# Attention, experts and MLP on one core: Strassen's scheme on two chunks of 320 tokens for seven expert blocks

## The chip, the cores and the metric

The kernel runs on one core of one Trainium2 chip. The metric is the device time of one execution in microseconds (us). The change is compared with the kernel before by the medians of several runs of each on one chip.

## The reference, cut to what matters

```python
# q, k, v: (2, 8, 576, 64)
scores = scale * q @ k.T + decay          # causal, decay from cumsum(log f)
x = softmax(scores) @ v                   # -> x: 1152 tokens x 512
p = domain_probs / domain_probs.sum(-1, keepdims=True)
for e in range(4):                        # experts, w1: 512 x 1024, w2: 1024 x 512
    out += p[:, e:e+1] * (np.maximum(x @ w1[e], 0) @ w2[e])
h = out @ w_in                            # w_in: 512 x 2048, w_out: 2048 x 512
y = (h * (1 / (1 + np.exp(-1.702 * h)))) @ w_out
```

All of it is wanted to float32 accuracy. The two MLP weights arrive as 64-bit floats; the others as float32.

## The kernel before, in words

**Products.** Each float32 operand is split into a rounded high part and the rest: `x` into `xh`, `xl`, a first-layer weight into `whi`, `wlo`, a hidden value into `hh`, `hl`. A product is then three passes of matmuls: high by high, low by high, high by low. `whi` and `hh` are rounded by ScalarE (ACT, the helper at L56), `wlo` is a subtraction on VectorE (DVE, L208).

**Blocks and visits.** The hidden units come in 12 blocks of 512: eight of the experts (0 to 7, two for each) and four of the MLP (8 to 11). `visits` lists which block goes over which chunks of tokens in which order. While attention still runs, visits 0 to 9 do blocks 2, 1, 0 and 3 on the four chunks that attention delivers (256, 256, 256 and 384 tokens). Visits 7, 8 and 9 are blocks 3, 1 and 0 on the last two of them, tokens 512 to 1151. Visits 10 to 17 are blocks 4 to 11 on three chunks of 384 (`WIDE`).

**Units.** `seq` lists units of work. Kind 1 is a plain first layer of a block on a chunk (`emit_l1`, L800): four steps of 12 matmuls. Kind 2 is the second layer (`emit_l2`, L914): per tile of 128 tokens 12 matmuls that are 512 wide, whose result DVE adds to `acc` (L925 for experts, L931 and L934 for the MLP). Kind 3 is half of a first layer of two chunks together by Strassen's scheme (`emit_joint`, L839): seven products of six matmuls where the plain way has eight. It needs sums of weights and sums of tokens. The sums of weights (`sr`) are four operations of POOL for each half (L224 to L227), split by `split_sums` into `sh` (ACT, two operations) and `sl` (DVE, L237, two operations). The pool `ws` holds one such pair. The sums of tokens are ten additions `tr` (L260), four roundings `th` (ACT) and four subtractions `tl` (L255); `sum_tokens` makes them twice, once for the experts (all additions on POOL, spread over visits 7 to 9) and once for the MLP (seven on DVE, three on POOL, in visit 14). In visits 10 to 13 and 15 to 17 the order is: half 0, the second layer left over from the visit before, half 1, the third chunk plainly, and the second layer of the first two chunks. Visit 14, the MLP's first, is plain, since its input is only just made: `split_output` transposes each finished tile on the PE (L1037) and splits it into `xh` and `xl` (L1043).

**After a product.** The first layer of an expert ends in `jc` (DVE, L844), a relu, `hh` (ACT) and `hl` (POOL, L848); that of the MLP in a gelu (ACT, L902), `hh` and `hl` (DVE, L904).

**MLP weights.** `mlp_convert` turns the 64-bit floats into float32, 32 tiles, each by six DVE operations (L313 to L327, on tiles `cvt`, `cvd`, `wf`). The result is stored to DRAM (`wm`, L340) and loaded again as `wst` (L62) when its block is due. `cv_due` sets how many of these steps go with each unit step.

**Order.** A scheduler orders the PE's instructions. From visit 10 on `pin_turn` fixes the order of DVE, ACT and POOL as the program emits it. These three engines and each DMA queue work in their order: an instruction that waits holds up all behind it.

Of the kernel before, what the change touches and what calls it, by code (L numbers as in the profile page):

```python
# [23 lines left out]
WN = 384  # L24
WIDE = [NCH, NCH + 1, NCH + 2]
# [5 lines left out]
TS_FROM, TS_EVERY = 7, 2  # L31
# [4 lines left out]
def attn_moe_mlp(ctx: ExitStack, tc: tile.TileContext, qk0, qk1, qk2, v0, vp, fg, dp, wa_moe, wb_moe, wa_mlp, wb_mlp, out):  # L36
# [34 lines left out]
    h_p = pool("h", 2)  # L71
# [68 lines left out]
    runs = [[v_ for v_, (b, cs) in enumerate(visits) if cs is WIDE and lo <= b < hi]  # L140
            for lo, hi in ((0, NMOE), (NMOE + 1, NBLK))]
    joint = runs[0] + runs[1]
    for run in runs:
        at = seq.index((1, run[0], visits[run[0]][0], WIDE[0]))
        ends = run[-1] + 1 == len(visits)
        to = len(seq) if ends else seq.index((1, run[-1] + 1, visits[run[-1] + 1][0], WIDE[0]))
        mid, before = [], seq[at + 1]
        for v_ in run:
            b = visits[v_][0]
            mid += [(3, v_, b, WIDE[0]), before, (3, v_, b, WIDE[1]), (1, v_, b, WIDE[2]), (2, v_, b, WIDE[0]), (2, v_, b, WIDE[1])]  # L150
            before = (2, v_, b, WIDE[2])
        seq[at:to] = mid + [before] * ends
    v8 = runs[0][-1] + 1
    ts_units = [(2, v8 - 1, NMOE - 1, WIDE[2]), (1, v8, NMOE, WIDE[1]), (2, v8, NMOE, WIDE[0])]
    last_unit = {v_: cs[-1] for v_, (b, cs) in enumerate(visits)}
# [85 lines left out]
    def sum_tokens(eng, eng3):  # L241

        (h11, h21, h12, h22), (l11, l21, l12, l22) = ([t[c][:, k:k + 2] for c in WIDE[:2] for k in (0, 2)] for t in (xh, xl))
        if not ts:
            th, tl = (late["ts"].tile([128, 4, 2, WN], F32R, name=n) for n in ("th", "tl"))
            ts.update({n: (th[:, n - 1], tl[:, n - 1]) for n in range(1, 5)})
            ts.update({11: (h11, l11), 21: (h21, l21), 22: (h22, l22)})
        ra, rb = (late["jr"].tile([128, 1024], F32, tag="jr", name="tr")[:, :2 * WN].rearrange("p (k n) -> p k n", k=2)
                  for _ in range(2))
# [19 lines left out]
        sub_, add_ = eng3.tensor_sub, eng3.tensor_add  # L269
# [13 lines left out]
    v_mlp = [v_ for v_, (b, _) in enumerate(visits) if b >= NMOE]  # L283
    m_order = [(k, v_, g) for v_ in v_mlp for k in "ab" for g in range(4)]
# [108 lines left out]
    def load_plain(h0):  # L393
# [394 lines left out]
    hbuf = {}  # L788

    def emit_l1(v_, b, c, g):  # L790
        n = span[c][1]
        if g == 0:
            hbuf[v_, c] = (h_p.tile([128, 4, WN], F32R, tag="hh", name="hh"),
                           h_p.tile([128, 4, WN], F32R, tag="hl", name="hl"))
        hh, hl = hbuf[v_, c]
# [33 lines left out]
    def emit_joint(v_, b, m):  # L829

        c1, c2 = WIDE[:2]
        for c, p in ((c1, h_p), (c2, late["h2"])) if m == 0 else ():
            hbuf[v_, c] = tuple(p.tile([128, 4, WN], F32R, tag=t, name=t) for t in ("hh", "hl"))
        (h1, l1), (h2, l2) = hbuf[v_, c1], hbuf[v_, c2]
# [61 lines left out]
    def evac_l1(b, n, g, hh, hl, p):  # L896
        if b < NMOE:
            nc.scalar.activation(out=hh[:, g, :n], in_=p[:, :n], func=AF.Relu)  # L898
            nc.vector.scalar_tensor_tensor(out=hl[:, g, :n], in0=p[:, :n], scalar=0.0, in1=f(hh[:, g, :n]),  # L899
                                           op0=ALU.max, op1=ALU.subtract)  # L900
# [4 lines left out]

    def emit_l2(v_, b, c, j):

# [4 lines left out]
        for i, (x, w) in enumerate([(hh, 0), (hh, 1), (hl, 0)]):
            for k in range(4):
                nc.tensor.matmul(p, lhsT=x[:, k, o], rhs=wb[v_, k][w].rearrange("p a c -> p (a c)"),  # L914
                                 start=(i == 0 and k == 0), stop=(i == 2 and k == 3))
        return lambda: evac_l2(v_, b, c, t, p)
# [280 lines left out]
```

## Time and profile before

| | us |
|---|---|
| runs | 702.04, 700.75, 701.94 (median 701.94) |
| the profiled execution | 699.91 |
| its span in the profile | 698.2 |
| PE busy in it | 686.4 (98%) |
| DVE busy in it | 493.3 (71%) |
| ACT, POOL busy in it | 326.3, 212.7 |

The span is that of the instructions of one execution; the execution's own time is 1.71 us longer. PE is TensorE, PEld its weight loads. A matmul's busy time in a timeline overlaps its neighbours'; the chain of waits gives the time that a run of matmuls really took.

### The profile page before, as it was taken

Reading aid. Unit: us, or ns where it says so; the run is one execution under the profiler, and the core shown is the slowest. Engines: PE = TensorE matmul, PEld = TensorE weight load, DVE = VectorE, ACT = ScalarE, POOL = GpSimd, SP = SyncE. Lnnn points to the kernel's source line nnn. Section 1 sums busy time; section 2 is a strip of 40 time slices with the busy share of each in tenths; the row PEclk is TensorE's granted clock in tenths of the full one; section 3 lists DMA queues with packets and bytes.
Section 4 is the critical chain, followed back from the end, with each engine's and each line's share of the span. In section 5 each row is a group of like instructions: output and inputs, shape, how many; then the busy total and the mean of one; then the engine's idle time right before and its main releaser. Section 6 shows DMA issues by size and latency. Waiting matters only on the chain.

```text
span 698.2 us, 10644 instructions
## 1 busy us (share of the span) xinstructions
PE 686.4 (98%) x3864; PEld 608.3 (87%) x3865; DVE 493.3 (71%) x1004; ACT 326.3 (47%) x737; POOL 212.7 (30%) x237
## 2 busy tenths in 40 slices
PE   8999999999999999999999999999989999999997
PEld 4797888888888998999899898897988898998986
DVE  6896776676486777657877679677876779684632
ACT  5777766676441342346045244352455453451430
POOL 6887566632260033015116025120043302100000
PEclk9999999999999999999999999999999999999999
DMA  7686735332323614413413343234103244110012
GB/s 260 232 288 242 271 118 190 127 92 92 121 61 107 209 50 163 107 45 114 143 55 127 121 134 104 95 121 150 46 18 117 77 152 152 45 61 31 0 46 91
DMA packets 38597, 83.37 MB, mean 119 GB/s; under 512 B 3560, under 2 KB 3568, under 8 KB 38544
## 3 DMA queue, kind: packets, MB, share of 16 engines
q1 hardware_dynamic: 38504, 82.65, 35.9%
q8 instruction: 30, 0.49, 0.3%
q14 instruction: 23, 0.19, 0.1%
q10 hardware_dynamic: 40, 0.04, 0.0%
HBM read 71.88 MB, written 10.78 MB: 118 GB/s over the span
## 4 chain that ended last, share of the span: by engine, by line
PE 95%; DVE 2%; POOL 1%; ACT 1%; DMA 1%; issue 0%; SPq 0%; POOLq 0%
PE m L914 42%; PE m L800 25%; PE m L839 15%; PE s L536 4%; PE x L640 4%; PE t L610 3%; DMA dpraw<-in_dp_dram 1%; DVE tr L260 0%; POOL ks L462 0%; PE m L1037 0%; PE m L817 0%; POOL e L592 0%; PE t L684 0%; PE m L953 0%; ACT xh L56 0%; POOL qlo L480 0%
## 5 line engine op out<-in xcount | busy, mean ns | idle before, releaser
L914 PE MATMUL m<-whi,hh 128*128 128x512 f32 x432 | 119.4, 392 | 0.0
L914 PE MATMUL m<-wlo,hh 128*128 128x512 f32 x432 | 117.1, 391 | 0.0
L914 PE MATMUL m<-whi,hl 128*128 128x512 f32 x432 | 116.3, 390 | 0.0
L208 DVE TENSOR_TENSOR wlo<-wst,whi 128x512 fp32r<-128x512 f32 x140 | 110.4, 806 | 4.8 <-ACT whi L56 4.3
L56 ACT ACTIVATE whi<-wst 128x512 fp32r<-128x512 f32 x144 | 85.9, 625 | 28.5 <-PE m L914 17.8
L914 PEld LDWEIGHTS m<-whi,hl 128*128 128x128 f32 x432 | 80.9, 188 | 17.1
L914 PEld LDWEIGHTS m<-wlo,hh 128*128 128x128 f32 x432 | 80.9, 188 | 17.0
L914 PEld LDWEIGHTS m<-whi,hh 128*128 128x128 f32 x432 | 79.7, 188 | 13.7
L800 PE MATMUL m<-xh,whi 128*128 128x384 f32 (+1 forms) x400 | 79.4, 315 | 2.6 <-ACT xh L56 2.6
L800 PE MATMUL m<-xh,wlo 128*128 128x384 f32 (+1 forms) x400 | 78.7, 313 | 0.0
L800 PE MATMUL m<-xl,whi 128*128 128x384 f32 (+1 forms) x400 | 78.6, 313 | 0.0
L800 PEld LDWEIGHTS m<-xh,whi 128*128 128x128 f32 x400 | 65.0, 189 | 4.9 <-ACT xh L56 3.3
L848 POOL TENSOR_TENSOR hl<-jc,hh 128x384 fp32r<-128x384 f32 x24 | 24.5, 1020 | 139.9 <-ACT hh L56 139.9
L800 PEld LDWEIGHTS m<-xh,wlo 128*128 128x128 f32 x400 | 65.1, 189 | 0.0
L800 PEld LDWEIGHTS m<-xl,whi 128*128 128x128 f32 x400 | 64.7, 189 | 0.3
L592 POOL TENSOR_SCALAR e<-e,sm 128x128 f32<-128x128 f32 (+4 forms) x72 | 46.0, 650 | 54.4 <-DVE sm L590 25.2
L898 ACT ACTIVATE hh<-m 128x256 fp32r<-128x256 f32 (+1 forms) x84 | 36.0, 428 | 55.1 <-PE m L800 55.0
L899 DVE SCALAR_TENSOR_TENSOR hl<-m,hh 128x256 fp32r<-128x256 f32 (+1 forms) x84 | 40.6, 483 | 29.5 <-ACT hh L898 28.9
L925 DVE SCALAR_TENSOR_TENSOR acc<-m,dpn,acc 128x512 f32<-128x512 f32 x63 | 47.0, 746 | 17.5 <-PE m L914 17.3
L904 DVE TENSOR_TENSOR hl<-m,hh 128x384 fp32r<-128x384 f32 x48 | 26.7, 555 | 32.6 <-ACT hh L56 32.5
L582 ACT ACTIVATE e<-e,mx 128x128 f32<-128x128 f32 (+4 forms) x72 | 41.6, 580 | 11.1 <-DVE mx L566 10.6
L902 ACT ACTIVATE m<-m 128x384 f32<-128x384 f32 x48 | 23.1, 481 | 39.5 <-DVE m L844 37.8
(142 smaller groups left out, 1147.3 us busy)
## 6 DMA issues: line engine op xcount, KB each, us to landing
wst<-in_wa_moe_dram SPq DMA_DIRECT2D x28, 512.0 KB, 4.4
wst<-in_wb_moe_dram SPq DMA_DIRECT2D x28, 512.0 KB, 4.2
mst<-in_wa_mlp_dram SPq DMA_DIRECT2D x16, 512.0 KB, 3.9
wm<-wf SPq DMA_DIRECT2D x32, 256.0 KB, 3.4
mst<-in_wb_mlp_dram SPq DMA_DIRECT2D x16, 512.0 KB, 4.0
wst<-wm SPq DMA_DIRECT2D x16, 512.0 KB, 3.8
cb<-cumd SPq DMA_DIRECT2D x16, 256.0 KB, 4.0
qr<-in_qk_dram SPq DMA_DIRECT2D x8, 384.0 KB, 5.4
```

The costliest lines, as they stand in the source:

```text
L56: return nc.scalar.activation(out=out, in_=in_, func=AF.Copy)
L208: (nc.gpsimd if v_ == 0 and kind == 'a' and g < 4 else nc.vector).tensor_sub(lf, raw, f(hf))
L536: nc.tensor.matmul(pt[:, :z - a], lhsT=lr[i][0], rhs=lr[i][1], start=i == 0 and not (both and pt is not bank), stop=i == n - 1, skip_group ...
L582: nc.scalar.activation(out=e[:, off:off + w], in_=e[:, off:off + w], func=AF.Exp, scale=-1.0, bias=mx, accum_out=sm[:, 0, k:k + 1])
L592: nc.gpsimd.tensor_scalar(out=e[:, off:off + w], in0=e[:, off:off + w], scalar1=sm[:, 0, i:i + 1], scalar2=1.0, op0=ALU.mult, op1=ALU.mult)
L640: nc.tensor.matmul(pt[64 * g:64 * g + 64, o:n], lhsT=lhsT, rhs=rhs, start=i == 0, stop=i == nk - 1)
L800: nc.tensor.matmul(p[:, :n], lhsT=w[:, k, :], rhs=x[c][:, k, :], start=(j == 0 and k == 0), stop=(j == 2 and k == 3))
L839: nc.tensor.matmul(p[:, :WN], lhsT=w[a][:, k, :], rhs=x[z][:, k, :], start=start and j == 0 and k == 0, stop=stop and j == 2 and k == 1, s ...
L898: nc.scalar.activation(out=hh[:, g, :n], in_=p[:, :n], func=AF.Relu)
L899: nc.vector.scalar_tensor_tensor(out=hl[:, g, :n], in0=p[:, :n], scalar=0.0, in1=f(hh[:, g, :n]), op0=ALU.max, op1=ALU.subtract)
L914: nc.tensor.matmul(p, lhsT=x[:, k, o], rhs=wb[v_, k][w].rearrange("p a c -> p (a c)"), start=(i == 0 and k == 0), stop=(i == 2 and k == 3))
L925: nc.vector.scalar_tensor_tensor(out=a, in0=p, scalar=d, in1=a, op0=ALU.mult, op1=ALU.add)
```

## The change

Visits 7, 8 and 9 become joint too, on two chunks of 320 tokens (512 to 831, 832 to 1151), and have no third chunk. Visits 10 to 13 use the same two chunks and do tokens 0 to 511 plainly as one chunk of 512 (`REST`). A new kind 4 (`emit_l2_joint`) does the second layer of the five tiles of the two chunks: first the parts of k = 0, 1 into five accumulators, then those of k = 2, 3. The MLP keeps chunks of 384 in a new order: joint are tokens 384 to 1151, plain are 0 to 383. Its first visit begins with tokens 768 to 1151. The last expert's tokens 0 to 511 finish after the others, its tiles in the order 3, 0, 1, 2. The sums of tokens are made once per 320-token pair and once per 384-token pair, now wholly on DVE: the experts' two steps at a time in the three last units of visit 6. Fewer conversion steps go with early units (`cv_due` 0.3 instead of 0.7), and 1.2 with each later one. The buffers of `hh`, `hl` become two tiles that `h_of` cuts up. `pin_turn` begins at visit 7.

```diff
-WIDE = [NCH, NCH + 1, NCH + 2]
+JN = 320
+LATE = [(384, WN), (768, WN), (0, WN), (S - 64, JN), (S - 64 + JN, JN), (0, S - 64)]
+MLP = [NCH, NCH + 1, NCH + 2]
+EXP = [NCH + 3, NCH + 4, NCH + 5]
+REST = EXP[2]
...
-    visits = [(2, [0]), (1, [0]), (0, [0]), (3, [0, 1]), (0, [1]), (1, [1]), (2, [1, 2, 3]), (3, [2, 3]), (1, [2, 3]), (0, [2, 3])]
-    visits += [(b, WIDE) for b in range(4, NBLK)]
+    visits = [(2, [0]), (1, [0]), (0, [0]), (3, [0, 1]), (0, [1]), (1, [1]), (2, [1, 2, 3])]
...
+    v_exp, v_all, v_mlp = len(visits), len(visits) + 3, len(visits) + 7
+    visits += [(b, EXP[:2]) for b in (3, 1, 0)] + [(b, EXP) for b in range(4, NMOE)] + [(b, MLP) for b in range(NMOE, NBLK)]
+    joint = [v_ for v_ in range(v_exp, len(visits)) if v_ != v_mlp]
...
+    before = []
+    for v_ in range(v_exp, len(visits)):
+        b, cs = visits[v_]
+        if v_ == v_mlp:
+            seq += before
+            seq += [(1, v_, b, cs[1]), (1, v_, b, cs[0]), (2, v_, b, cs[1]), (1, v_, b, cs[2]), (2, v_, b, cs[0])]
+            before = [(2, v_, b, cs[2])]
+            continue
+        seq += [(3, v_, b, cs[0])] + before + [(3, v_, b, cs[1])]
+        seq += [(1, v_, b, c) for c in cs[2:]]
+        seq += [(4, v_, b, cs[0])] if b < NMOE else [(2, v_, b, cs[0]), (2, v_, b, cs[1])]
+        before = [(2, v_, b, c) for c in cs[2:]]
+    seq += before
+    sums_at = {(1,) + units[-1]: 2, (2,) + units[-2]: 2, (2,) + units[-1]: 2}
+    sums_at.update({(1, v_mlp, NMOE, MLP[0]): 2, (2, v_mlp, NMOE, MLP[1]): 2, (1, v_mlp, NMOE, MLP[2]): 1, (2, v_mlp, NMOE, MLP[0]): 1})
...
-    def sum_tokens(eng, eng3):
+    def sum_tokens(cs):
...
+        eng, width = nc.vector, span[cs[0]][1]
...
-        sub_, add_ = eng3.tensor_sub, eng3.tensor_add
...
     def emit_l2(v_, b, c, j):
...
+        if c == REST:
+            j = (3, 0, 1, 2)[j]
...
+    def emit_l2_joint(v_, b, c, j):
+
+        if j < 5:
+            both.append(ps_tile())
+            l2_products(v_, b, c, j, both[j], (0, 1))
+            return lambda: None
+        p = both[j - 5]
+        l2_products(v_, b, c, j - 5, p, (2, 3))
+        if j == 9:
+            both.clear()
+        return lambda: evac_l2(v_, b, c, span[c][0] // 128 + j - 5, p)
...
-            ts_gen = sum_tokens(nc.gpsimd, nc.gpsimd)
-        if (kind, v_, b, c) == ts_units[0]:
-            ts_gen = sum_tokens(nc.vector, nc.gpsimd)
+            ts_gen = sum_tokens(EXP)
+        u, m = (kind, v_, b, c), visits[v_][1].index(c)
+        if u == (1, v_mlp, NMOE, MLP[0]):
+            ts_gen = sum_tokens(MLP)
...
-                if (kind, v_, b, c) not in ts_units:
-                    cv_due[0] += (0.7 if v_ < 10 else 0.5 if kind == 3 else 1.4 if b >= NMOE else 1.3) * (4 / n_steps)
+                if sums_at.get(u, 0) < 2:
+                    cv_due[0] += (0.3 if v_ < v_all else 1.2) * (4 / n_steps)
...
-            if v_ >= 10:
+            if v_ >= v_exp:
                 pin_turn()
```

How the order of instructions moves, at three places. Rows are line, operation, result and operands, shape, and how many stand in a row. The changed kernel's lines are its own: L837 is the plain first layer, L874 the joint one, L950 the second layer, L1094 the transposes.

**PE, from half 0 to half 1 of the first joint visit.** Before (visit 10), from the last product of half 0:

```order
L839 MATMUL m<-xl,sh 128x384 x2
L914 MATMUL m<-whi,hh 128x512
L914 MATMUL m<-wlo,hh 128x512 x4
L914 MATMUL m<-whi,hl 128x512 x4
L914 MATMUL m<-whi,hh 128x512 x4
L914 MATMUL m<-wlo,hh 128x512 x4
L914 MATMUL m<-whi,hl 128x512 x4
L839 MATMUL m<-xh,whi 128x384 x2
L839 MATMUL m<-xh,wlo 128x384 x2
L839 MATMUL m<-xl,whi 128x384 x2
L839 MATMUL m<-th,sh 128x384 x2
```

Changed (visit 7), from the last rows of half 1's first product, which now stands ahead of half 0's last:

```order
L874 MATMUL m<-xl,whi 128x320 x2
L874 MATMUL m<-xh,sh 128x320 x2
L874 MATMUL m<-xh,sl 128x320 x2
L874 MATMUL m<-xl,sh 128x320 x2
L874 MATMUL m<-th,sh 128x320 x4
L950 MATMUL m<-whi,hh 128x512 x2
L950 MATMUL m<-wlo,hh 128x512 x2
L950 MATMUL m<-whi,hl 128x512 x2
L874 MATMUL m<-th,sh 128x320 x2
L874 MATMUL m<-th,whi 128x320 x2
```

Before, 21 second-layer matmuls of another visit and the next first product stand between the last use of one `sh` and the first use of the next. Now they follow each other directly, and behind four matmuls come six of this visit's own second layer.

**PE, from the last expert to the MLP.** Before, from the transposes of tile 1:

```order
L1037 MATMUL m<-identr,acc_79 128x128 x4
L914 MATMUL m<-whi,hh 128x512 x4
L914 MATMUL m<-wlo,hh 128x512 x4
L914 MATMUL m<-whi,hl 128x512 x4
L1037 MATMUL m<-identr,acc_79 128x128 x4
L800 MATMUL m<-xh,whi 128x384 x4
L800 MATMUL m<-xh,wlo 128x384 x4
L1037 MATMUL m<-identr,acc_79 128x128 x4
L800 MATMUL m<-xh,whi 128x384 x4
L800 MATMUL m<-xh,wlo 128x384 x4
```

Changed, from the transposes of tile 8 on:

```order
L1094 MATMUL m<-identr,acc_2863 128x128 x4
L950 MATMUL m<-whi,hh_2861 128x512 x4
L950 MATMUL m<-wlo,hh_2861 128x512 x4
L950 MATMUL m<-whi,hl_2862 128x512 x4
L1094 MATMUL m<-identr,acc_79 128x128 x8
L837 MATMUL m<-xh,whi 128x384 x4
L837 MATMUL m<-xh,wlo 128x384 x4
L837 MATMUL m<-xl,whi 128x384 x4
```

Before, the MLP's first layer reads tiles 0 to 2, and the transposes of tile 2 stand right ahead of it. Now it reads tiles 6 to 8, and behind the last of their transposes come a tile's second layer and the transposes of two other tiles.

**DVE, the last conversions.** Before, from the last conversion step (L327) to visit 17's first `u`:

```order
L327 TENSOR_TENSOR wf<-wf,cvd 128x512
L904 TENSOR_TENSOR hl<-m,hh 128x384
L208 TENSOR_TENSOR wlo<-wst,whi 128x512
L237 TENSOR_TENSOR sl<-sr,sh 128x512 x2
L904 TENSOR_TENSOR hl<-m,hh 128x384
L208 TENSOR_TENSOR wlo<-wst,whi 128x512
L931 TENSOR_TENSOR acc_79<-m,acc_79 128x512
L208 TENSOR_TENSOR wlo<-wst,whi 128x512
L931 TENSOR_TENSOR acc_79<-m,acc_79 128x512 x4
L931 TENSOR_TENSOR acc_2876<-m,acc_2876 128x512
L867 TENSOR_TENSOR u_6960<-m,u_6960 128x384
L874 TENSOR_TENSOR u_6961<-m,u_6960 128x384
```

Changed, from the middle of visit 17's half 0 to the first `u` of its half 1:

```order
L880 TENSOR_TENSOR m<-u_7026,m 128x384
L944 TENSOR_TENSOR hl_2862<-m,hh_2861 128x384
L342 TENSOR_SCALAR cvt<-wf 128x512
L257 TENSOR_TENSOR sl<-sr,sh 128x512 x2
L880 TENSOR_TENSOR m<-m,u_7025 128x384
L944 TENSOR_TENSOR hl<-m,hh 128x384
L345 SCALAR_TENSOR_TENSOR cvd<-mst,cvt 128x512
L347 TENSOR_TENSOR wf<-wf,cvd 128x512
L988 TENSOR_TENSOR acc_79<-m,acc_79 128x512 x3
L228 TENSOR_TENSOR wlo<-wst,whi 128x512
L903 TENSOR_TENSOR u_7157<-m,u_7157 128x384
```

The last conversion stood ten rows ahead of visit 17; now the last three steps lie within its first half.

## Rows read from the trace of the kernel before

**Rows 1.** The page: span, two engines, granted TensorE clock in slices.
```profile
span 698.2 us, 10644 instructions
...
PE 686.4 (98%) x3864; PEld 608.3 (87%) x3865; DVE 493.3 (71%) x1004; ACT 326.3 (47%) x737; POOL 212.7 (30%) x237
...
PEclk9999999999999999999999999999999999999999
```

**Rows 2.** Chain of waits, 180 to 345 us: start, length, line, instructions.
```profile
199.37 8.34 PE m L800 x48
207.72 5.48 PE m L914 x24
213.20 5.75 PE m L800 x48
...
296.50 6.26 PE m L839 x36
...
306.20 1.06 PE m L839 x6
307.27 4.80 PE m L914 x21
```

**Rows 3.** Who PE waited for, 200 to 698 us: total, times, longest.
```profile
PE m L800 <- ACT xh L56: 2.6, 2, 1.9
```

**Rows 4.** Timeline of PE, 485 to 523 us: start, length, and idle before.
```profile
488.85 0.97 PE L800 MATMUL m<-xh,whi 128*128 128x384 f32 x4 [0.69 <-ACT xh L56]
...
520.06 0.97 PE L800 MATMUL m<-xh,whi 128*128 128x384 f32 x4 [1.95 <-ACT xh L56]
```

**Rows 5.** Timeline of ACT, 485 to 523 us.
```profile
517.77 0.84 ACT L56 ACTIVATE th<-tr 128x768 fp32r<-128x768 f32 x1 [4.51 <-DVE tr L260]
```

**Rows 6.** Timeline of DVE, 485 to 523 us.
```profile
499.95 0.95 DVE L260 TENSOR_TENSOR tr<-xh 128x768 f32<-128x768 f32 x1
...
515.15 2.59 DVE L260 TENSOR_TENSOR tr<-tr,xl 128x768 f32<-128x768 f32 x1
```

**Rows 7.** Timeline of POOL, 485 to 523 us.
```profile
514.76 4.66 POOL L260 TENSOR_TENSOR tr<-tr,xl 128x768 f32<-128x768 f32 x2
```

**Rows 8.** Timeline of ACT, 302 to 313 us.
```profile
307.37 1.16 ACT L56 ACTIVATE sh<-sr 128x512 fp32r<-128x512 f32 x2 [1.31 <-PE m L839]
```

**Rows 9.** Timeline of DVE, 304 to 313 us.
```profile
308.45 1.29 DVE L237 TENSOR_TENSOR sl<-sr,sh 128x512 fp32r<-128x512 f32 x2
```

**Rows 10.** Busy time of each engine in three stretches.
```profile
194.00:221.40 27.40, 27.40 (x156) 25.05 (x155) 23.69 (x33) 10.39 (x22) 9.52 (x5) 1.00 0.34 106
...
344.06:391.62 47.56, 47.56 (x241) 43.23 (x241) 36.59 (x62) 18.50 (x36) 14.16 (x14) 1.00 0.34 107
...
591.32:638.88 47.56, 47.56 (x241) 43.23 (x241) 32.59 (x59) 19.50 (x40) 2.92 (x4) 1.00 0.15 52
```

**Rows 11.** DVE groups, 543 to 640 us: busy, mean ns, idle before.
```profile
L904 DVE TENSOR_TENSOR hl<-m,hh 128x384 fp32r<-128x384 f32 x24 | 13.3, 555 | 13.6 <-ACT hh L56 13.6
L208 DVE TENSOR_TENSOR wlo<-wst,whi 128x512 fp32r<-128x512 f32 x17 | 12.2, 725 | 0.0
L931 DVE TENSOR_TENSOR acc<-m,acc 128x512 f32<-128x512 f32 x15 | 10.2, 684 | 5.7 <-PE m L914 5.7
L327 DVE TENSOR_TENSOR wf<-wf,cvd 128x512 f32<-128x512 f32 x8 | 6.4, 805 | 0.1
...
L237 DVE TENSOR_TENSOR sl<-sr,sh 128x512 fp32r<-128x512 f32 x8 | 5.2, 687 | 2.6 <-ACT sh L56 2.6
```

**Rows 12.** Busy time of the instructions on tile cvt in one stretch.
```profile
543.76:591.32 47.56, 14.07 (x23) 2.65 (x4) 1.00 0.39 135
```

**Rows 13.** Timeline of DVE, 192 to 200 us.
```profile
194.65 5.55 DVE L208 TENSOR_TENSOR wlo<-wst,whi 128x512 fp32r<-128x512 f32 x3
```

**Rows 14.** The page: DMA issues, KB each, median us to landing.
```profile
wm<-wf SPq DMA_DIRECT2D x32, 256.0 KB, 3.4
...
wst<-wm SPq DMA_DIRECT2D x16, 512.0 KB, 3.8
```

More of the change, by code (lines that the diff above doesn't have):

```diff
@@ L77, in attn_moe_mlp @@
     xh_t, xl_t = (big.tile([128, 4, NT], F32R, name=n) for n in ("xh", "xl"))
-    span = [(0, 256), (256, 256), (512, 256), (768, 384)] + [(i * WN, WN) for i in range(3)]
+    span = [(0, 256), (256, 256), (512, 256), (768, 384)] + LATE
     xh, xl = ([t[:, :, t0:t0 + n] for t0, n in span] for t in (xh_t, xl_t))
@@ L139, in attn_moe_mlp @@
     seq.append((2,) + units[-1])
[L140 to L155, printed above, removed]
+    before = []
[13 more added lines that the diff above has]
+    sums_at.update({(1, v_mlp, NMOE, MLP[0]): 2, (2, v_mlp, NMOE, MLP[1]): 2, (1, v_mlp, NMOE, MLP[2]): 1, (2, v_mlp, NMOE, MLP[0]): 1})
+    last_l1, last_l2 = {}, {}
+    for u in seq:
+        (last_l1 if u[0] in (1, 3) else last_l2)[u[1]] = u
     w_turn = [("a", 0), ("b", 0)]
-    for kind, v_, b, c in seq:
-        if c == last_unit[v_] and v_ + 1 < len(visits):
-            w_turn.append(("ab"[kind - 1], v_ + 1))
+    for u in seq:
+        if u[1] + 1 < len(visits) and u in (last_l1[u[1]], last_l2[u[1]]):
+            w_turn.append(("ab"[u[0] in (2, 4)], u[1] + 1))
     w_pairs = [(k, v_, g) for k, v_ in w_turn for g in (0, 2)]
@@ L282, in attn_moe_mlp @@
     wm = pool("wm", 1, bass.MemoryType.DRAM).tile([32, 128, 512], F32, name="wm")
[L283 to L284 removed]
+    m_order = [(k, v_, g) for v_ in range(v_mlp, len(visits)) for k in "ab" for g in range(4)]
     m_raw = {}
@@ L376, in begin_late @@
         late["rs"] = pool("rs", 1)
+        hbuf[0] = tuple(late["h2"].tile([128, 4, WN], F32R, name=n) for n in ("hh2", "hl2"))
         acc.append(late["rs"].tile([128, 4, 512], F32, name="acc1"))
@@ L398, in load_plain @@
         else:
-            qd, kd = (h_p.tile([128, 4 * WN], F32, tag=t, name=n)[:, :G * wk] for n, t in (("qd", "hh"), ("kd", "hl")))
+            qd, kd = (scratch(i, 4 * WN)[:, :G * wk] for i in range(2))
         qd, kd = (t.rearrange("p (g s) -> p g s", g=G) for t in (qd, kd))
@@ L829, in emit_joint @@
     def emit_joint(v_, b, m):
[L831 to L834, printed above, removed]
+        c1, c2 = visits[v_][1][:2]
+        WN = span[c1][1]
         def product(p, w, x, start, stop):
@@ L906, in emit_l2, with l2_products @@
+    def l2_products(v_, b, c, j, p, ks):
+        for i, (x, w) in enumerate([(0, 0), (0, 1), (1, 0)]):
+            for k in ks:
+                nc.tensor.matmul(p, lhsT=h_tile(v_, b, c, j, x, k), rhs=wb[v_, k][w].rearrange("p a c -> p (a c)"),
+                                 start=i == 0 and k == 0, stop=i == 2 and k == 3)
     def emit_l2(v_, b, c, j):
-        t = tiles(c)[j]
-        hh, hl = hbuf[v_, c]
-        o = slice(128 * j, 128 * j + 128)
+        if c == REST:
+            j = (3, 0, 1, 2)[j]
@@ L911, in emit_l2 @@
         p = ps_tile()
[L912 to L916, printed above, removed]
+        l2_products(v_, b, c, j, p, range(4))
+        return lambda: evac_l2(v_, b, c, tiles(c)[j], p)
+    both = []
+    def emit_l2_joint(v_, b, c, j):
[8 more added lines that the diff above has]
+        return lambda: evac_l2(v_, b, c, span[c][0] // 128 + j - 5, p)
```

131 lines of the change are left out of this document (81 added, 50 removed).

## Prediction

> **What bounds the kernel now.** I read the page first: the PE is busy in 98% of the span at the full granted clock of 2.4 GHz in all 40 slices [rows 1]. So time can come from two places only: fewer or narrower matmuls, or the few waits of the PE. The chain of waits gives what a matmul costs where nothing stops it [rows 2]: 48 of 384 columns in 8.34 us are 173.8 ns each, 48 of 256 in 5.75 us are 119.8, 24 of 512 in 5.48 us are 228.3. The three lie on a line, 54 ns for 128 columns, so I take 146.8 ns for 320, the middle of the first two. Next I asked who the PE waited for after attention: only for ACT's `xh`, twice, 2.6 us together [rows 3]. Both waits are where the MLP begins [rows 4].
>
> **The change part by part.**
>
> *Matmuls, visits 7 to 9.* The second layer keeps its matmuls, 12 for each tile. The first layer of such a visit had 48 of 256 columns and 48 of 384, 14.09 us; two joint halves have 84 of 320, 12.33 us. That is 1.76 less for each of three visits: -5.28.
>
> *Matmuls, visits 10 to 13.* Before, 84 joint and 48 plain matmuls of 384: 132 x 173.8 = 22.94 us. Now 12.33 and 48 of 512, 10.96: 23.29. That is 0.35 more for each of four visits: +1.40. The sum of the two is **-3.9 us**. The MLP's widths stay. The three widths fit their line within 1 ns, so this term is good to about 0.6 us.
> By the Trainium skill (TensorE: Matmul & The Clock Gate, Back-to-back issue gap) a warm matmul takes N / 2.4 GHz + 2.5 ns. The rows have some 11 ns more at each width (109 against 119.8 at 256), so they decide; by the page the two terms would be -4.9 and +1.3, an estimate of -3.6.
>
> *Where the MLP begins.* The two waits are 0.69 and 1.95 us [rows 4]. The first is the split of tile 2, whose transposes stand right ahead of the MLP's first matmuls. The second ends a chain: ACT waited 4.51 us for `tr` [rows 5], which DVE made in 2.59 us [rows 6] while POOL made two other `tr` in 4.66 [rows 7]; the same addition takes 0.95 alone. In the change the MLP begins with tiles 6 to 8, behind whose last transposes a tile's second layer (12 x 228 ns = 2.7 us) and eight more transposes stand, against an `xh` of 0.61 us and an `xl` of 0.69; the tiles that finish last are read last. And POOL adds no tokens any more. I take both waits as gone: **-2.6 us**. The ends are -2.6 and, if DVE with its ten additions is late for another tile, a new wait of the longest that is seen here, +1.9.
>
> *Halves without cover.* `ws` holds one pair of sums. In visit 10 of before, half 0's last product ends at 307.27; ACT then splits `sh` for half 1 from 307.37 on, two operations in 1.16 us [rows 8], and DVE `sl` in 1.29 [rows 9]. The PE has 4.80 us of second layer meanwhile [rows 2]. In visits 7 to 10 that unit is gone. By the order of instructions nothing stands in that place in visit 7, five second-layer matmuls (1.1 us) in visit 8, ten (2.3) in visit 9, twelve plain ones (2.7) in visit 10. The first `sh` takes about 0.6 and a 0.1 of delay: 0.7 us of wait in visit 7, and some 0.3 in visit 8, whose five must themselves wait for `hh` and `hl` of that half. `sl` comes later, behind work enough. I take **+1.0 us**. The lower end is 0; the upper one, with nothing of it covered at four places, is 4 x (0.10 + 1.16 + 1.29) = 10.2.
>
> *The experts' token sums.* They now have to be made between the last tokens (about 194.6 us) and the joint start, at 221.4 (207.72 + 5.48 + 36 x 0.228, the first layer before them unchanged [rows 2]); the third sum is first read three products later, at 224.0. Ten `tr` and four `tl` at 0.95 x 640/768 = 0.79 us are 11.1 us. With them DVE has 7 evictions into `acc`, 5 `wlo`, 4 `hl`, 2 `sl` there, by rows 11 another 12.0. That is 23.1 of 29.4 us, where DVE before was busy for 23.7 of 27.4 [rows 10]. Nothing on the path: 0. The cover is thin, see the rivals.
>
> *DVE after that.* Each of visits 7 to 9 has 12.33 us of first layer and 60 second-layer matmuls, 13.7: 26.0 us of PE. Its DVE work by rows 11 is 8 `wlo` 5.8, 4 `sl` 2.7, 5 evictions 3.4, and twelve `u`, sums of products and `hl` of 320 columns at 0.46 each, 5.6: 17.5 us, and with one conversion of 3.9 some 21.4. In visits 10 to 13 DVE had 36.6 of 47.56 us [rows 10]; one conversion more in each makes 40.5 of 47.9. It stays below the PE: 0.
>
> *Late conversions.* Visit 16 now has six of them, before two to three. Its DVE work is, by rows 11: 12 `hl` 6.7, 9 `acc` 6.2, 8 `wlo` 5.8, 4 `sl` 2.7, ten `u` and sums of products at the price of `hl`, 5.6; and six conversions of 3.86 us each (five steps of 0.61 [rows 12] and one of 0.805), 23.2. That is 50.2 us in 47.56, where it was 32.6 [rows 10]. DVE leaves this visit 2.6 us late, and more where it waits for a reload. Visit 17 has one conversion and its last weights are read in the second layer, some 30 us in, so the PE should feel little: 0 to 0.5, taken as 0.
>
> The sum is -3.9 - 2.6 + 1.0 = **-5.5 us**. The profiled execution took 699.91, its successor would take 694.4. The median of the runs lies 2.03 above the profiled one: **696.4 us**.
>
> **The rivals.**
>
> *A. Only the matmuls count.* The waits at the MLP's start come back as others: DVE does there ten additions where it did seven, and pays for POOL's sums of weights beside them. For it: those additions hold ACT's `th`, and ACT's `xh` stands behind it. Against it: the transposes lie earlier. Time: 701.9 - 3.9 + 1.0 = 699.0.
>
> *B. DVE becomes the bound from 194 us on.* Three `wlo` took 5.55 us beside POOL's additions [rows 13], 1.85 each against 0.725 [rows 11], 2.6 times as long. Eight sums of weights, 1.0 us each on POOL (14 in 14.16 [rows 10]), now lie beside the token sums. If each slows DVE so, it loses 8.1 x (1 - 1/2.6) = 5.0 us: 28.1 us of work from 194.6 end at 222.7, close to the 224.0. With the work of visits 7 to 9 slowed in like manner, I price this at 1 us at the start and 0.7 at each of four halves more than taken: 696.4 + 3.8 = 700.2. Against it: the means that I used already hold such hindrance.
> The Trainium skill (GPSIMD Engine Reference, Key points) says that POOL shares its SBUF interfaces with DVE where DVE reads two inputs; rows 6, 7 and 13 agree. By that rule the move of the additions off POOL also helps DVE, which the sum leaves out.
>
> *C. Slower: late conversions stop ACT and DVE in order.* A converted pair goes to DRAM (3.4 us) and back (3.8) [rows 14], and ACT's `whi` of that pair stands in the queue ahead of gelus that the PE's accumulators wait for. If visit 16 meets two such trips unhidden, DVE enters visit 17 late by 2.6 + 2 x 7.2 = 17 us. The PE can run about one half ahead before it has no free accumulator, 36 products in 6.26 us [rows 2]. It would stand 17 - 6.3 = 10.7 us: 707.1. It decides from a lateness of about 13 us, where a stall of 7 eats the gain. For it: visit 16 is over full, and in visit 17 conversion steps lie between the evictions. Against it: the PE gives each visit 47.56 us, and by the order only one of the trips lies open for some 4 us, which makes a lateness of 6 to 7.
>
> **How the numbers follow.** A measurement of this kernel can tell about 0.2%, 1.4 us, from no change. The forecast (694 to 698.5) has 0.66, A 0.13, B 0.13, C 0.08. The likeliest gives 696.4. Faster by over 1.4 us: the forecast, A, and B but for its worse end, 0.83; within it: 0.09, from B and from a mild C; slower: 0.08, from C. The range goes from the sum without new waits, 695.4, less the 1.3 us by which the runs differ, rounded to 693.8, to just past B, 700.6.
>
> **What would show it.** Right: joint matmuls every 147 ns; periods of 26.0 us in visits 7 to 9 and 47.9 in visits 10 to 13; no wait of the PE for `xh` over 0.3 us; a wait for `sh` under a microsecond in visit 7. Wrong: waits for `tl` or `th` at 221 us, a DVE without idle time over whole visits, waits for `sl` at the halves, or a PE idle in visit 17 for `hl` or `whi` of late weights.

## The result, and the profile after

| | us |
|---|---|
| the changed kernel, runs | 711.28, 707.53, 709.95, 710.55 (median 710.25) |
| the kernel before beside it, four runs | median 701.35 |
| ratio | 1.0121, interval 1.0097 to 1.0146 |
| profiled execution of the change | 711.28, span 709.6 |

The change is 1.2% slower. The forecast was 696.4 with a range to 700.6. The page of the changed kernel, answering to [rows 1]:

```profile
span 709.6 us, 10711 instructions
...
PE 690.4 (97%) x3829; PEld 599.3 (84%) x3829; DVE 507.4 (72%) x1057; ACT 342.2 (48%) x789; POOL 218.7 (31%) x266
```

The span grew by 11.4 us, PE's busy time by 4.0. So most of the loss is time in which the PE stands. The chain of waits shows where; below, the last piece ahead of the first joint half, the first pieces of visits 11, 12, 13, 15 and 16, and the last piece of all:

```profile
208.29 13.64 PE m L950 x60
...
349.83 5.28 PE m L874 x36
...
397.59 5.28 PE m L874 x36
...
445.35 5.28 PE m L874 x36
...
549.58 6.26 PE m L874 x36
...
597.14 6.26 PE m L874 x36
...
682.80 23.18 PE m L950 x102
```

The first joint half starts at 221.93, where 221.4 was forecast. Visits 11 and 12 take 47.76 us each, where 47.9 was forecast, and 36 matmuls of 320 columns take 5.28 us: 146.7 ns each, where 146.8 was interpolated. From 445.35 to 549.58, visit 13 and the MLP's first, nothing is lost. Two stretches are longer than their matmuls:

- 221.93 to 349.83 (visits 7 to 10, visit 10 without its leftover second layer). The matmuls need 3 x 26.0 + 37.0 = 115.0 us; it takes 127.9. **12.9 us are lost.**
- Visit 16 to the end, 597.14 to 705.98: 108.8 us. The kernel before takes 103.3 for the same matmuls, from 591.32 [rows 10] to the end of the piece below. **5.5 us are lost.**

```profile
670.08 24.54 PE m L914 x108
```

Busy time in the first stretch and in the second's last part (PE, PEld, DVE, ACT, POOL, granted clock, DMA):

```profile
221.93:349.83 127.90, 120.53 (x626) 105.68 (x626) 85.00 (x145) 58.45 (x124) 50.76 (x56) 0.97 0.29 87
...
644.70:706.00 61.30, 57.77 (x277) 49.22 (x275) 37.67 (x67) 17.49 (x37) 0.85 (x2) 1.00 0.21 73
```

In visits 7 to 10 the PE stands for 7.4 us, and DVE is busy for only two thirds. Who the PE waited for, where before there was only `xh` [rows 3] (the longest `hl` wait is of the end):

```profile
PE m L837 <- DVE u L910: 2.2, 1, 2.2
PE m L950 <- ACT hh L59: 1.9, 2, 1.4
PE m L874 <- ACT sh L59: 1.9, 1, 1.9
PE m L874 <- DVE hl L944: 1.8, 2, 1.5
```

The two waits for `xh` are gone.

**The turn of a visit.** The chain of waits from visit 7 to visit 8, from the last eviction of the second layer:

```profile
252.75 0.03 DVE acc L982
...
253.42 0.68 DVE wlo L228
254.10 0.40 DVE u L903
...
255.44 0.60 DVE wlo L228
256.04 0.41 DVE u L910
...
256.54 0.50 DVE jc L880
...
257.07 0.48 ACT jc L882
...
257.57 0.47 ACT hh L59
258.04 0.33 ACT hh L940
...
258.81 0.49 DVE jc L880
...
259.32 0.48 ACT jc L882
...
259.82 0.48 ACT hh L59
...
260.34 2.08 PE m L950 x4
```

This is the working of half 0: `u`, `jc`, relu, `hh`, a second `hh`, the next `jc`, its relu, its `hh`. DVE reaches the first `u` at 254.10, after five evictions and beside three `wlo`. Each step is an instruction of half a microsecond whose start waits for another engine's end, and each queue takes them in order. The PE is through with half 0's products at 258.2. One matmul of the second layer has its `hh` at 258.42, the next gets its own only at 260.34.

All four stops of this stretch lie in half 0 or right behind it: 1.9 us in visit 7, 1.6 in visit 8, 1.7 in visit 9 (in four pieces), 2.2 in visit 10. Each is for another link of the same working. In visit 7 it is `sh` by name, but ACT had relu and `hh` of half 0 ahead of it in its queue. In visit 10 the matmul that waits is a plain one, so other matmuls were at hand. It reads only `xh` and `whi`; that `u` has to empty an accumulator for it is the likely reason, and no view shows it.

```profile
230.83 0.85 PE L874 MATMUL m<-th,sh 128*128 128x320 f32 x4 [1.87 <-ACT sh L59]
...
317.22 1.19 PE L837 MATMUL m<-xh,whi 128*128 128x512 f32 x4 [2.21 <-DVE u L910]
```

```profile
230.16 1.13 ACT L59 ACTIVATE sh<-sr 128x512 fp32r<-128x512 f32 x2
```

Behind the stop in visit 8 the clock falls (the columns as above):

```profile
258.00:260.00 2.00, 0.73 (x3) 0.19 (x1) 0.89 (x2) 1.02 (x4) 0.87 (x1) 1.00 0.63 177
260.00:262.00 2.00, 1.66 (x4) 1.39 (x5) 1.16 (x2) 1.33 (x3) 0.87 (x1) 0.58 0.35 133
262.00:264.00 2.00, 2.00 (x8) 1.81 (x8) 1.38 (x3) 1.15 (x3) 0.13 (x1) 0.57 0.00 0
```

For about 3.4 us from 260.4 the granted clock is half, the 1.2 GHz level, right after 1.6 us of standing with one matmul between; the same happens from 318 on after 2.2 us. Each costs 1.7 us, so the clock takes 3.4 us of the stretch. The rest of the 12.9, some 2 us, is in time that counts as busy: a matmul that stands alone is 0.5 us long (0.49 at 258.42), where one in a full run costs 228 ns. With eight stops and parts of stops that makes 2 us, an estimate.

**The end.** The chain in visit 16, store and reload of a converted pair (compare [rows 14]), and DVE's next instruction in its timeline:

```profile
635.21 2.62 DMA wm<-wf
...
637.90 4.40 DMA wst<-wm
...
642.87 0.66 ACT cvt L332
...
643.54 0.62 DVE cvt L333
```

```profile
643.54 0.61 DVE L333 TENSOR_SCALAR cvt<-cvt 128x512 f32<-128x512 f32 x1 [4.92 <-ACT cvt L332]
```

DVE stood 4.92 us for ACT, whose rounding of late weights (`whi`) waited for the reload at the head of its queue. Behind that, DVE works without a gap from 643.5 to 658; three conversions end only at 651.9, 657.4 and 669.3, after the PE has begun visit 17. A second store and reload opens there, and DVE stands again:

```profile
675.93 0.69 DVE L228 TENSOR_TENSOR wlo<-wst,whi 128x512 fp32r<-128x512 f32 x1 [3.17 <-ACT whi L59]
```

The PE waits for `hl`, `acc` and sums of products, five times and 3.4 us in all.

### The profile page after: what moved, and what is told of

The parts are those of the page before. It is cut to its first block, busy times and chain, and to the rows that moved or that the text cites. A ratio compares the mean times of both kernels' runs of the same rounds, so it can differ in the third digit from the quotient of the medians.

```text
span 709.6 us, 10711 instructions
## 1 busy us (share of the span) xinstructions
PE 690.4 (97%) x3829; PEld 599.3 (84%) x3829; DVE 507.4 (72%) x1057; ACT 342.2 (48%) x789; POOL 218.7 (31%) x266
## 4 chain that ended last, share of the span: by engine, by line
PE 77%; DVE 9%; ACT 4%; DMA 4%; issue 3%; POOL 2%; SPq 0%; DVEq 0%; POOLq 0%; ACTq 0%
PE m L950 35%; PE m L837 18%; PE m L874 12%; PE s L558 4%; PE x L662 4%; PE t L632 3%; DVE wlo L228 2%; DMA wst<-wm 1%; ACT hh L59 1%; DMA wst<-in_wa_moe_dram 1%; DVE hl L944 1%; ACT m L935 1%; DVE acc L982 1%; DMA wm<-wf 1%; DVE cvd L345 1%
## 5 line engine op out<-in xcount | busy, mean ns | idle before, releaser
L950 PE MATMUL m<-whi,hh 128*128 128x512 f32 x432 | 126.2, 395 | 3.1 <-ACT hh L59 1.9
L950 PE MATMUL m<-whi,hl 128*128 128x512 f32 x432 | 123.2, 392 | 0.0
L950 PE MATMUL m<-wlo,hh 128*128 128x512 f32 x432 | 122.9, 392 | 0.0
L228 DVE TENSOR_TENSOR wlo<-wst,whi 128x512 fp32r<-128x512 f32 x140 | 105.7, 771 | 13.1 <-ACT whi L59 12.6
L950 PEld LDWEIGHTS m<-wlo,hh 128*128 128x128 f32 x432 | 81.2, 188 | 16.8
L950 PEld LDWEIGHTS m<-whi,hh 128*128 128x128 f32 x432 | 79.4, 188 | 18.8 <-ACT hh L59 2.6
L950 PEld LDWEIGHTS m<-whi,hl 128*128 128x128 f32 x432 | 80.9, 188 | 16.4
L884 POOL TENSOR_TENSOR hl<-jc,hh 128x320 fp32r<-128x320 f32 x42 | 37.3, 888 | 186.2 <-ACT hh L59 186.2
L244 POOL TENSOR_TENSOR sr<-wst 128x256 f32<-128x256 f32 x20 | 18.3, 916 | 168.5 <-DMA wst<-wm 81.7
L882 ACT ACTIVATE jc<-jc 128x320 f32<-128x320 f32 x42 | 19.8, 472 | 101.6 <-DVE jc L880 101.6
L837 PE MATMUL m<-xh,whi 128*128 128x256 f32 (+2 forms) x304 | 64.3, 328 | 2.2 <-DVE u L910 2.2
L837 PE MATMUL m<-xh,wlo 128*128 128x256 f32 (+2 forms) x304 | 65.3, 328 | 0.0
L837 PE MATMUL m<-xl,whi 128*128 128x256 f32 (+2 forms) x304 | 65.0, 329 | 0.0
L837 PEld LDWEIGHTS m<-xh,whi 128*128 128x128 f32 x304 | 50.2, 189 | 5.9 <-DVE u L910 2.5
L941 DVE SCALAR_TENSOR_TENSOR hl<-m,hh 128x384 fp32r<-128x384 f32 (+2 forms) x82 | 35.9, 438 | 26.7 <-ACT hh L940 26.2
L837 PEld LDWEIGHTS m<-xl,whi 128*128 128x128 f32 x304 | 50.8, 191 | 2.9
L837 PEld LDWEIGHTS m<-xh,wlo 128*128 128x128 f32 x304 | 50.9, 190 | 2.6
L257 DVE TENSOR_TENSOR sl<-sr,sh 128x512 fp32r<-128x512 f32 x40 | 28.4, 748 | 24.7 <-ACT sh L59 24.6
```

Source lines behind the costliest of these rows:

```text
L228: (nc.gpsimd if v_ == 0 and kind == 'a' and g < 4 else nc.vector).tensor_sub(lf, raw, f(hf))
L257: nc.vector.tensor_sub(ls[:, o:o + 512], raw[:, o:o + 512], f(hs[:, o:o + 512]))
L837: nc.tensor.matmul(p[:, :n], lhsT=w[:, k, :], rhs=x[c][:, k, :], start=(j == 0 and k == 0), stop=(j == 2 and k == 3))
L884: nc.gpsimd.tensor_sub(hl[:, g, :], r, f(hh[:, g, :]))
L941: nc.vector.scalar_tensor_tensor(out=l_, in0=q, scalar=0.0, in1=f(h_), op0=ALU.max, op1=ALU.subtract)
L950: nc.tensor.matmul(p, lhsT=h_tile(v_, b, c, j, x, k), rhs=wb[v_, k][w].rearrange("p a c -> p (a c)"), start=i == 0 and k == 0, stop=i == 2 ...
```

## The experiments

They stand in the order in which they ran. Each is compared with the kernel before on the same chip, whose median there was 701.4 to 702.0.

**e1_conv: more conversions from visit 10 on.**

```diff
-cv_due[0] += (0.3 if v_ < v_all else 1.2) * (4 / n_steps)
+cv_due[0] += (0.3 if v_ < v_all else 1.5) * (4 / n_steps)
```

> The changed kernel took 710.25 us in the median, and its last three visits lost 5.5 us against the kernel before. Edit: 1.5 instead of 1.2 conversion steps with each later unit. Theory (the conversions come too late and hold up VectorE and ScalarE in visits 16 and 17): the loss goes, 704.5 to 706.5 us, with visit 15's start no later and the stretch from visit 16's start to the end near 103.5 us instead of 108.9. Rival (the MLP's new order of chunks, or the joint halves themselves, make that loss): within 1 us of 710.25, the stretch stays at 108 to 109.

Measured: 712.48 us, ratio 1.0159 (1.0132 to 1.0186). The end did get shorter, but the visits ahead of it took that back:

```profile
490.00:495.00 5.00, 2.78 (x16) 1.93 (x15) 4.97 (x8) 0.60 (x1) 3.64 (x4) 1.00 0.77 253
...
600.90:650.12 49.22, 48.39 (x242) 43.15 (x241) 35.78 (x64) 19.54 (x40) 4.01 (x5) 1.00 0.20 65
650.12:706.00 55.88, 55.72 (x276) 49.65 (x275) 23.70 (x41) 15.45 (x32) 0.00 (x0) 1.00 0.10 38
```

From visit 16's start (600.90) to 706 it is 105.1 us instead of 108.9. Visit 16 began 3.8 us later, though. At 490 to 495, where the MLP begins, DVE is busy for 4.97 of 5 us and the PE for 2.78: it waits 2.2 us for `acc` ahead of the transposes, and the clock falls behind that. The expected time was missed. At that rate the visits up to the MLP have no room for the conversions that the early ones no longer make.

**e2_early: weights split ahead of the turn.**

```diff
+                if kind == 4 and v_ < v_all:
+                    if 4 <= g < 8:
+                        split_q.append(("b", v_ + 1, g - 4))
-                if u == last_l2[v_] and g == n_steps - 1:
+                elif u == last_l2[v_] and g == n_steps - 1:
```

> Edit: in visits 7 to 9 the second-layer weights of the next visit are split while the second layer runs, no longer at the turn to the next visit; VectorE has the same work in another order. Theory (at the turns of visits 8, 9 and 10 the evacuations of the first products stand behind three to four of these subtractions in VectorE's queue, and the PE, with no second layer left as cover, waits for that chain): the chain gets some 2 us shorter at three turns, and the PE's clock does not fall there, 703 to 707 us. Rival (VectorE has simply too much work in visits 7 to 10): no change, 709 to 711.5 us.

Measured: 712.74 us, ratio 1.0157 (1.0135 to 1.0178), idle time of the PE between 196 and 350 us 8.7 instead of 7.4. My theory missed: at the turn to visit 8 `u` now stands right behind the last eviction, but the `wlo` between the evictions delay them: the last begins at 255.84, and `u` at 256.50.

**e3_plain: visits 7 to 9 plain.**

```diff
-    joint = [v_ for v_ in range(v_exp, len(visits)) if v_ != v_mlp]
+    joint = [v_ for v_ in range(v_all, len(visits)) if v_ != v_mlp]
...
-        seq += [(3, v_, b, cs[0])] + before + [(3, v_, b, cs[1])]
+        k1 = 3 if v_ in joint else 1
+        seq += [(k1, v_, b, cs[0])] + before + [(k1, v_, b, cs[1])]
```

> Edit: visits 7 to 9 do their first layers plainly again, on the two chunks of 320 tokens; all else as changed. The matmuls cost 5.3 us more. Theory (the joint halves without a second layer between them make the loss of 12.9 us between 222 and 350 us): some 9 to 10 us of it go, the share of visit 10 stays, 705 to 707 us. Rival (the loss comes from the two-part second layer, the token sums or the conversions, which stay): 714 to 716 us.

Measured: 704.57 us, ratio 1.0043 (1.0028 to 1.0058), a little better than the theory gave. The matmuls cost 5.3 us more and it is 5.7 us faster: the joint halves of three visits cost 11 us in waits and in what follows a wait. Idle time up to 350 us is 0.8, all of it in visit 10; the end still loses 3.7.

**e6_wsplit: two of the four weight sums split early.** `split_sums` makes two pairs of tiles, each when its old content is done with:

```diff
-            for o in (0, 512):
-                round_act(hs[:, o:o + 512], raw[:, o:o + 512])
-                nc.vector.tensor_sub(ls[:, o:o + 512], raw[:, o:o + 512], f(hs[:, o:o + 512]))
+            round_act(hs, raw[:, 512 * i:512 * i + 512])
+            nc.vector.tensor_sub(ls, raw[:, 512 * i:512 * i + 512], f(hs))
+            part.append((sh, sl))
```

> Edit: the four sums of weights of a half lie in two pairs of tiles, so that two of them can be split while the half before still uses the other two; the second half's products then come ahead of the first half's last one. Theory of the single buffer (the PE waits at the halves because the pair of sums is still in use): 1.9 us in visit 7 and as much in visits 8 to 10 in sum go, 705 to 707.5 us. Rival (it waits for the evacuations of the half before, hh and jc, in the queues of ScalarE and VectorE): the wait moves to the second layer's first hh, less than 1.5 us of gain, 708.5 to 711.

Measured: 710.91 us, ratio 1.0134 (1.0119 to 1.0149); idle time up to 350 us 7.9. The rival held. The wait for `sh` is gone and others have its place (`sl` 3.7, `hh` 1.9, `jc` 1.9). The single buffer, which my forecast priced, is not the cause: in visit 10 ACT has the first pair's `sh` (here `sha`) done at 311.0, and its `sl` starts in DVE's queue only at 316.69.

```profile
310.37 0.63 ACT L59 ACTIVATE sha<-sr 128x512 fp32r<-128x512 f32 x1 [0.17 <-POOL sr L246]
```

```profile
316.69 0.68 DVE L257 TENSOR_TENSOR sla<-sr,sha 128x512 fp32r<-128x512 f32 x1
```

**e4_mlp: the kernel before, with only the MLP's start covered.**

```diff
+    x = seq.index((2, v8 - 1, NMOE - 1, WIDE[2]))
+    y = seq.index((1, v8, NMOE, WIDE[0]))
+    seq[x], seq[y] = seq[y], seq[x]
-    ts_units = [(2, v8 - 1, NMOE - 1, WIDE[2]), (1, v8, NMOE, WIDE[1]), (2, v8, NMOE, WIDE[0])]
+    ts_units = [(1, v8, NMOE, WIDE[1]), (2, v8, NMOE, WIDE[0]), (1, v8, NMOE, WIDE[2])]
```

> The kernel before with one edit: the last expert's second layer on tokens 768 to 1151 comes ahead of the MLP's first plain chunk instead of behind it, and the MLP's token sums begin one unit later. Matmuls and their widths stay. Theory (the term of 2.6 us of the forecast: with second-layer work between the transposes and the MLP's first matmuls both waits for xh go): 698.3 to 699.5 us, no wait of the PE for xh over 0.3 us. Rival (the wait comes back with another tile or behind the token sums): 700.8 to 702.5.

Measured: 697.39 us, ratio 0.9937 (0.9925 to 0.995), faster than forecast. In the trace, from visit 10's start to visit 15's it is 244.1 us instead of 247.3: the two waits of 2.6 us, and 0.5 behind them. The other 1.4 us of the 4.6 between the medians are not in the trace. The granted clocks of the runs say where most of it may lie: the ten runs of the kernel before have a mean of 0.9978, these five 0.9996. Of some 700 us that is 1.5 and 0.3, an estimate. In the stretch where before the PE stood twice it is now never idle:

```profile
490.00:541.00 51.00, 51.00 (x271) 46.55 (x270) 38.03 (x55) 27.84 (x54) 14.35 (x11) 1.00 0.20 62
```

**e8_noconv: no conversions in visits 7 to 9.**

```diff
-(0.3 if v_ < v_all else 1.2)
+(0 if v_exp <= v_ < v_all else 0.3 if v_ < v_exp else 1.2)
```

> The changed kernel with no conversion steps in visits 7 to 9 (they come later). Theory (in visits 7 to 10 the PE waits for a chain of operations from engine to engine, one half directly behind the other, whatever VectorE's load): idle time of the PE between 222 and 350 us stays at 6 to 8 us, as in the runs so far (7.4 in the changed kernel, 8.7 with the weights split earlier). Rival (VectorE has too much work there): with some 2 us less for it in each visit the idle time falls under 4 us. The whole takes 709 to 714 by the theory, since the conversions pile up at the end, and 704 to 709 by the rival.

Measured: 722.0 us, ratio 1.0291 (1.0274 to 1.0307). Idle time up to 350 us is 5.5, just under what the theory gave and well above the rival's 4; it fell all the same, from 7.4. The end loses far more than expected, and the forecast for the whole missed: one stop of 14.0 us for `hl` at the start of visit 17; ahead of it stand a store of 3.94 and a reload of 4.42 us in the chain.

**e10_plainconv: e3_plain with early conversions.**

```diff
-(0.3 if v_ < v_all else 1.2)
+(0.93 if v_ < v_all else 1.2)
```

> The plain visits 7 to 9 of e3_plain (704.57 us), and 0.93 instead of 0.3 conversion steps with each unit step there, which is the kernel before's number for a visit. Theory (what e3_plain still loses at its end, some 5.5 us, is that too few conversions are made before visit 10): 699 to 701.5 us. Rival (that loss belongs to the MLP's new order of chunks): 704 to 705.5.

Measured: 699.28 us, ratio 0.9968 (0.9955 to 0.9981). From visit 15's start on the PE waits for nothing. The loss at the end belonged to the conversions.

**e11_nocover: the kernel before, leftover second layer ahead of half 0.**

```diff
-            mid += [(3, v_, b, WIDE[0]), before, (3, v_, b, WIDE[1]), (1, v_, b, WIDE[2]), (2, v_, b, WIDE[0]), (2, v_, b, WIDE[1])]
+            mid += [before, (3, v_, b, WIDE[0]), (3, v_, b, WIDE[1]), (1, v_, b, WIDE[2]), (2, v_, b, WIDE[0]), (2, v_, b, WIDE[1])]
```

> The kernel before with one edit: in visits 10 to 13 and 15 to 17 the second layer left over from the visit before comes ahead of half 0 instead of between the halves, so that the two joint halves follow each other directly; all else stays, the plain visits 7 to 9 too. Theory (it is the missing cover between the halves that makes the PE wait): 0.7 to 1.9 us are lost in each of seven visits, 706 to 714 us. Rival (the halves need no cover; the loss is due to what else the change brought into visits 7 to 10, two-part second layers and fuller queues): 701 to 703.5.

Measured: 710.68 us, ratio 1.0135 (1.0112 to 1.0157). One move of a unit makes the kernel before as slow as the change. The PE's waits for `sh`, and the boundary of the halves in visit 12 in the chain of waits:

```profile
PE m L839 <- ACT sh L56: 6.8, 3, 2.5
```

```profile
400.37 7.30 PE m L839 x42
407.68 1.56 PE m L800 x9
409.24 1.04 PE m L839 x6
410.28 2.60 PE m L800 x15
```

Only three of seven boundaries stall (visits 13, 15 and 16). In visits 10 to 12 the scheduler put plain matmuls of the third chunk (L800) between the products. In visit 17 twelve of them stand ahead of the new `sh`. In visits 13, 15 and 16 it put none there. The last product of half 0 in visit 13, the next matmul, and what ACT did meanwhile:

```profile
455.68 0.51 PE L839 MATMUL m<-xl,sh 128*128 128x384 f32 x2
458.12 0.97 PE L839 MATMUL m<-th,sh 128*128 128x384 f32 x4 [1.92 <-ACT sh L56]
```

```profile
457.02 0.52 ACT L56 ACTIVATE hh<-jc 128x384 fp32r<-128x384 f32 x1
457.45 1.14 ACT L56 ACTIVATE sh<-sr 128x512 fp32r<-128x512 f32 x2
```

The PE was done with the old `sh` at 456.2. ACT rounds the new one only at 457.45, behind a relu that waited for DVE's `jc`, and its `hh`. So here too the wait for `sh` is mostly for half 0's working. The two stalls behind it are followed by 1.2 GHz as well, 3.2 us of loss in all. So what decides is what the PE can do in between, not that the halves are neighbours in the program.

**e12_half: half of each early visit joint, the other half plain.** Kind 5 is the plain half: four steps of 12 matmuls. Conversions as in e10_plainconv.

```diff
-        seq += [(3, v_, b, cs[0])] + before + [(3, v_, b, cs[1])]
+        seq += [(3, v_, b, cs[0])] + before + [(5 if v_ < v_all else 3, v_, b, cs[1])]
...
+                ev = emit_l1(v_, b, EXP[g % 2], 2 + g // 2) if kind == 5 else {1: emit_l1, 2: emit_l2, 4: emit_l2_joint}[kind](v_, b, c, g)
```

> The version with early conversions (e10_plainconv, 699.28 us) with half of each early visit joint again: in visits 7 to 9 half 0 by Strassen's scheme, the other half plainly, so that 48 plain matmuls stand behind half 0 as cover and no second pair of weight sums is needed. Matmuls: 42 + 48 of 320 columns are 13.2 us against 14.1, 0.88 less in each of three visits. Theory (a joint half is free of waits where enough other matmuls stand behind it): 696.2 to 697.3 us, idle time of the PE between 222 and 350 us under 1.5. Rival (the turn of a visit stalls any joint half that follows the two-part second layer): a wait of 1 to 2 us in each of the three visits, 699.5 to 703.

Measured: 695.2 us, ratio 0.9911 (0.9894 to 0.9928), the fastest of all, a little better than the theory gave, 6.4 us under the kernel before and some 4 under e10_plainconv. From 200 us on the PE waits for nothing. Visits 7 to 10 (columns as above):

```profile
221.40:340.00 118.60, 118.60 (x651) 107.07 (x650) 89.08 (x156) 51.82 (x110) 37.94 (x39) 1.00 0.36 118
```

DVE is busy for 89.1 of 118.6 us here, 75%, and in the changed kernel for 85.0 of 127.9. It does more work in less time and the PE does not wait. The edit does two things at once: it gives half 0 its cover, and it takes away half 1's joint working with its pair of weight sums.

**e13_conv93: the change with early conversions.** The edit of e10_plainconv, on the changed kernel.

> The changed kernel with 0.93 instead of 0.3 conversion steps in the early visits, joint halves and all else as changed. Theory (two separate losses: the missing cover in visits 7 to 10, and the late conversions at the end): the loss at the end goes (5.5 us), the one in visits 7 to 10 stays or grows by a little through VectorE's fuller queue: 704 to 707.5 us, idle time of the PE under 1 us from visit 16 to the end, 7 to 10 us between 222 and 350. Rival (conversions beside the early joint halves cost as much there as they save at the end): 709 to 712.

Measured: 718.81 us, ratio 1.0247 (1.0222 to 1.0273): theory and rival both too low. The end is without a wait, as the theory had it, but the early stretch lost nearly twice as much as in the change:

```profile
221.40:360.47 139.07, 123.75 (x626) 108.02 (x625) 97.56 (x168) 60.43 (x128) 51.33 (x56) 0.94 0.31 101
...
607.79:655.35 47.56, 47.56 (x241) 43.23 (x241) 35.32 (x65) 20.07 (x41) 2.92 (x4) 1.00 0.24 78
655.35:711.00 55.65, 55.65 (x276) 49.63 (x275) 23.57 (x40) 15.45 (x32) 0.00 (x0) 1.00 0.10 38
```

There the PE stands for 15.3 us and the mean clock is 0.94. Without conversions beside the joint halves it stood 5.5 (e8), with 0.3 a step 7.4, with 0.93 15.3.

## Why the prediction was wrong, point by point

The sum was -5.5 us; against the span before it came out at +11.4. Of the 16.9 between them, 11.9 lie in visits 7 to 10, 5.5 at the end, 0.5 came before the first joint half, and visits 11 to 15 were 1 us better than forecast. The forecast of the median missed by 13.9 only, and the difference is luck: I put the median 2.03 above the profiled execution, and here it lies 1.03 below it.

- **Matmuls, -3.9 us: right.** 146.7 ns at 320 columns, periods of 47.76 us.
- **Where the MLP begins, -2.6: right**, in the change and alone (e4_mlp). Rival A's return of the waits did not come.
- **Halves without cover, +1.0: the step that failed.** It measured +12.9. I priced one thing that needs the cover, the split of `sh` and `sl` behind the last use of the buffer [rows 8, 9], and took it to begin as soon as the buffer is free. The cover also hid the whole working of half 0 through DVE, ACT and POOL. In visit 7 the wait for `sh` was 1.87 us, where 0.7 was forecast, and stops of like size came in visits 8 to 10. e6_wsplit took the priced wait away and gained nothing; e11_nocover took the cover away from the kernel before and lost 8.7; e3_plain and e12_half have no joint half without cover in visits 7 to 9 and no stop there. The upper end that I wrote beside the term, 10.2, was nearer, and that it lay above the whole gain should have been a rival.
- **DVE stays below the PE, 0: true and beside the point.** 85 of 128 us is no bound. What counts is how long `u` and `jc` stand in DVE's queue when the PE needs them next: e13_conv93 adds 12.6 us of DVE work to the stretch (97.6 against 85.0) and the PE's idle time doubles; without conversions in visits 7 to 9 (e8_noconv) 5.5 us of it stay.
- **The 1.2 GHz stretches** were in no term. They cost 3.4 us in the profiled execution. They don't come in each execution: the run of 707.53 us had a mean clock of 1.000, the one of 711.28 had 0.995, which is 3.5 us of 709.6.
- **Late conversions, 0: wrong.** They cost 5.5. This was rival C's mechanism, with the place and the queue that it named. Its price of 10.7 was too high: it let two whole trips of 7.2 us lie open in visit 16, and DVE stood for 4.92 us there and 3.17 in visit 17. I counted 50 us of DVE work in visit 16 and then let visit 17 take the lateness for nothing. e10_plainconv and e13_conv93 show the end without a wait once the conversions are made early.
- **The experts' token sums, 0: right.** The first joint half began when the matmuls ahead of it were done.
- Rival B had the stretch, but its price of 0.7 for a half was set by DVE's amount of work. That work counts where the cover is gone (e13_conv93), and e12_half, with more of it, has no stop.

What stays open: which link of half 0's working would have to be shortened, since e2_early and e6_wsplit each took one and another took its place; why some stops are followed by 1.2 GHz and others are not; and what of e4_mlp's gain lies outside its trace.

## What to carry to other kernels

When a unit of work between two dependent stages is removed, price the whole chain that it hid, instruction by instruction through every in-order queue, and not the one buffer that is reused; a busy share of 66% says nothing of it. A saving in matmuls is worth having where other matmuls can stand behind it: against plain visits 7 to 9, half of the scheme with cover (e12_half against e10_plainconv) gained some 4 us, and all of it without cover (the change against e3_plain) lost 5.7. Work that is taken from a full queue early has to be placed elsewhere; look at the queue where it lands.

## What the runs showed of the hardware

A stop of the PE of 1.6 to 2.5 us was sometimes followed by some 3.4 us at 1.2 GHz and sometimes not: in the changed kernel behind those that end at 260.34 and 317.22, not behind that of 1.87 us that ends at 230.83; in e1_conv behind none of three stops of like length in visits 7 to 10, but behind those that end at 493.35 and 494.61 (1.61 and 0.60 us). So a short stall can cost twice its length, and executions of the same program differ: 711.28 us at a mean clock of 0.995 and 707.53 at 1.000. The kernel before shows the same. Of its eleven runs beside e12_half the four with a mean clock of 0.999 or more took 699.88 to 700.21 us, the seven with less 701.57 to 703.44.
